# An attention-and-Hyena kernel on one core: issue order decided by a list scheduler for all five engines

## The chip, the cores and the metric

The kernel runs on one core of one Trainium2 chip. The metric is the device time of one execution in microseconds (us). The kernel before takes 576.78 us, the median of three runs from 569.41 to 578.04.

The engines are PE (TensorE: matrix products), PEld (the loading of its weights, which overlaps PE: in 451.6 us of the kernel before, the middle below, PE is busy for 376.4 us and PEld for 154.1, more than 451.6 together), DVE (VectorE), ACT (ScalarE), POOL (GpSimd) and SP (which issues most DMAs here).

## The reference, cut to what matters

```python
# q, k, v: [4 batches, 8 heads, 768, 64]
def _attn_ref(q, k, v, centroids):
    q_assign = argmax(normalised(q) @ normalised(centroids).T)     # 16 clusters
    k_assign = argmax(normalised(k) @ normalised(centroids).T)
    mask = q_assign[:, :, :, None] == k_assign[:, :, None, :]
    scores = where(mask, q @ k.T / 8, -1e9)
    attn = exp(scores - max);  attn = attn / (sum(attn) + 1e-9)
    return attn @ v

def _moe_ref(x, w_proj, filter_fft, w_out):    # "Hyena" below
    x1, x2, x3 = split(x @ w_proj)             # 512 -> 3 * 512
    x2_conv = irfft(rfft(x2) * rfft(filter_fft))
    return (x1 * x2_conv * x3) @ w_out
```

(The `einsum` and `matmul` calls are written as `@`.) The heads' outputs, side by side, are the `x` of the second part. The transform is done by matrix products with tables of sines and cosines ("the tables").

Four kinds of work follow. *Routing* finds the clusters of eight groups (a group is half a batch's heads). *Attention* has 16 pairs of heads with six steps each, thus 96 steps; a step is two score products, two exponentials on ACT, eight value matmuls on PE and two running sums on DVE. A *denominator* closes each pair. *Hyena* runs once for each of the four batches, when that batch's attention is done. Routing and Hyena are laid between the attention steps as *filler*.

## The kernel before

The kernels use PSUM, into which PE writes, as eight banks. The pools take two pairs of banks for scores, one pair for the values and two single banks for all filler:

```python
    psS = ctx.enter_context(tc.tile_pool(name="psS", bufs=2, space=PSUM))
    psO = ctx.enter_context(tc.tile_pool(name="psO", bufs=1, space=PSUM))
    psF = ctx.enter_context(tc.tile_pool(name="psF", bufs=2, space=PSUM))
    # ... (cut)
    def bank():
        return psF.tile([128, 512], F32, name="pf")
    # ... (cut)
        def scores(self, sk, hp):
            K = 80 if hp == 0 else 128
            sps = psS.tile([128, 2, 512], F32, name="ps")
            for ch in range(2):
                nc.tensor.matmul(sps[:, ch, :384], ...)                # cut
            # ... (cut)
            nc.scalar.activation(p[:, :S]..., sps[:, :, :384], Act.Exp, scale=0.125)
```

A filler group is a handful of matmuls into one bank, and then a copy out of it. This is the first of Hyena's:

```python
        for m in range(3):
            for e in range(2):
                ps = bank()
                for kt in range(ND):
                    nc.tensor.matmul(ps, uvf[:, e, kt, ts(m, 128)], wpj[:, kt, DM:2 * DM],
                                     start=(kt == 0), stop=(kt == ND - 1))
                nc.scalar.copy(uv2[:, e, m], ps)
                yield
```

Only PE's order is laid down by hand. Twelve steps share the filler that stands ready at their start, by counting:

```python
    for i, (n, pr, sk) in enumerate(steps):
        # ... (cut: which filler is added)
        left = sum(f[1] for f in fill)
        nf = -(-left // (12 - w)) if left else 0
        # ... (cut)
        scores(i + 1, 0)
        emit((nf + 1) // 2)
        scores(i + 1, 1)
        emit(nf // 2)
        if sk == 0 and i:
            pairs[steps[i - 1][:2]].finish()      # the denominator, through DRAM
        pairs[n, pr].values(sk)
```

The softmax here doesn't subtract the row's maximum and nothing guards it: scores larger than these inputs give would overflow.

Of the kernel before, what the change touches and what calls it, by code (L numbers as in the profile page):

```python
# [2 lines left out]

# [15 lines left out]










@with_exitstack  # L30
def kernel(
# [13 lines left out]
    B, H, S, D = q.shape  # L45
    NC = centroids.shape[1]
    DM = moe_w_proj.shape[0]
    assert (B, H, S, D, NC) == (4, 8, 768, 64, 16)
    assert DM == H * D
    NT = S // 128  # L50
    HS = S // 2
    ND = DM // 128
    BIG = 262144.0
    EPS = 1e-30

    consts = ctx.enter_context(tc.tile_pool(name="consts", bufs=1))
    psS = ctx.enter_context(tc.tile_pool(name="psS", bufs=2, space=PSUM))
    psO = ctx.enter_context(tc.tile_pool(name="psO", bufs=1, space=PSUM))
    psF = ctx.enter_context(tc.tile_pool(name="psF", bufs=2, space=PSUM))
    dram = ctx.enter_context(tc.tile_pool(name="dram", bufs=2, space=bass.MemoryType.DRAM))  # L60

    def bank():
        return psF.tile([128, 512], F32, name="pf")


    raw = ctx.enter_context(tc.tile_pool(name="raw", bufs=4))
    vraw = ctx.enter_context(tc.tile_pool(name="vraw", bufs=2))
    qk_raws, v_raws = {}, {}

    def load_qk(n, pr, j):  # L70
        if n < 2 * B:
            tl = qk_raws[n, pr, j] = raw.tile([128, NT, 2, D], F32, name="qkraw")
            for hp in range(2):
                nc.sync.dma_start(tl[:, :, hp], (q, k)[j][n // 2, 4 * (n % 2) + 2 * pr + hp].rearrange(
                    "(p t) d -> p t d", t=NT))

    def load_v(b, g):
        vv = v_raws[b, g] = vraw.tile([128, 4, 384], F32, name="vraw")
        nc.sync.dma_start(vv, v[b, 4 * g:4 * g + 4].rearrange("h (p t) d -> p h (t d)", t=NT))

    for z in range(4):
        load_qk(0, z // 2, z % 2)
    load_v(0, 0)


    ident = consts.tile([128, 128], F32)
    make_identity(nc, ident)
    identb = consts.tile([128, 128], BF16)
    nc.vector.tensor_copy(identb, ident)
    ones32 = consts.tile([128, 32], F32)  # L90
    nc.gpsimd.memset(ones32, 1.0)

    cbd = consts.tile([128, 4, 32], F32)
    nc.gpsimd.memset(cbd, 0.0)
    cen = ctx.enter_context(tc.tile_pool(name="cen", bufs=1))
    c = cen.tile([128, D], F32)
    nc.scalar.dma_start(c, centroids.rearrange("h c d -> (h c) d"))
    c2 = cen.tile([128, D], F32)
    nc.vector.tensor_tensor(c2, c, c, op=Alu.mult)
    ss = cen.tile([128, 1], F32)  # L100
    nc.vector.tensor_reduce(ss, c2, axis=AX, op=Alu.add)
    nc.vector.tensor_scalar(ss, ss, 1e-30, None, op0=Alu.max)
    s0 = cen.tile([128, 1], F32)
    nc.scalar.activation(s0, ss, Act.Sqrt)

    s1 = cen.tile([128, 1], F32)
    nc.vector.reciprocal(s1, s0)
    nc.vector.tensor_tensor(s1, s1, ss, op=Alu.mult)
    nc.vector.tensor_tensor(s1, s1, s0, op=Alu.add)
    nc.vector.tensor_scalar(s1, s1, 0.5, 1e-6, op0=Alu.mult, op1=Alu.add)  # L110
    nc.vector.reciprocal(s1, s1)
    cn = cen.tile([128, D], F32)
    nc.vector.tensor_scalar(cn, c, s1, None, op0=Alu.mult)
    cps = bank()
    nc.tensor.transpose(cps[:D, :128], cn, ident)
    cv = cps[:D, :128].rearrange("d (r e c) -> d r e c", r=4, e=2)
    nc.vector.tensor_copy(cbd[:D, :, :NC], cv[:, :, 0])
    nc.vector.tensor_copy(cbd[D:, :, NC:], cv[:, :, 1])


    mka = consts.tile([128, 1], F32)
    mkb = consts.tile([128, 1], F32)
    for g in range(4):
        nc.gpsimd.memset(mka[32 * g:32 * g + 32], BIG if g % 2 == 0 else 1.0)
        nc.gpsimd.memset(mkb[32 * g:32 * g + 32], -BIG if g % 2 == 0 else 0.0)

    revc = consts.tile([128, 48, NC], BF16)
    nc.gpsimd.iota(revc, pattern=[[0, 48], [-1, NC]], base=NC, channel_multiplier=0,
                   allow_small_or_imprecise_dtypes=True)



    NSET = 2
    augs = [[[[consts.tile([128, S], BF16, name=f"aug{i}{pr}{hp}{j}") for j in range(2)]
              for hp in range(2)] for pr in range(2)] for i in range(NSET)]
    for i in range(NSET):
        for pr in range(2):
            for j in range(2):
                nc.gpsimd.memset(augs[i][pr][1][j][:D], 0.0)


    NP = 6
    pbuf = [consts.tile([128, S + 4], F32, name=f"p{i}") for i in range(NP)]
    for p in pbuf:
        nc.gpsimd.memset(p[:, S:S + 1], EPS)
    np_ = [0]

    wpj = consts.tile([128, ND, 3 * DM], BF16)
    wout = consts.tile([128, ND, DM], BF16)


    fw = [consts.tile([128, 3, HS], BF16, name=f"fw{i}") for i in range(2)]
    inv = consts.tile([128, 6, HS], BF16)
    hm = consts.tile([128, 3, 4, DM], BF16)

    def forward_tables():
        with tc.tile_pool(name="tabw", bufs=1) as tab:
            s0 = tab.tile([128, 1], F32)
            nc.gpsimd.iota(s0, pattern=[[0, 1]], base=0, channel_multiplier=6,
                           allow_small_or_imprecise_dtypes=True)  # L160
            nc.vector.tensor_scalar(s0[64:], s0[64:], -383.0, None, op0=Alu.add)
            kc = tab.tile([128, 2, HS], F32)
            sh = tab.tile([128, 2, HS], F32)
            for i in range(2):
                nc.gpsimd.iota(kc[:, i], pattern=[[0, 2], [2, 192]], base=i, channel_multiplier=0,
                               allow_small_or_imprecise_dtypes=True)
                nc.gpsimd.memset(sh[:, i, :192], 192.0)
                nc.gpsimd.memset(sh[:, i, 192:], 0.0)
            nc.gpsimd.memset(kc[:, 0, 192:193], 384.0)
            nc.gpsimd.memset(sh[:, 0, 192:193], 192.0)  # L170
            MAGIC = 12582912.0
            for m in range(3):
                sm = tab.tile([128, 1], F32, bufs=2)
                nc.vector.tensor_scalar(sm, s0, float(2 * m), None, op0=Alu.add)
                n = tab.tile([128, 2, HS], F32, bufs=2)
                nc.vector.scalar_tensor_tensor(n, kc, sm, sh, op0=Alu.mult, op1=Alu.add)
                r = tab.tile([128, 2, HS], F32, bufs=2)
                nc.vector.tensor_scalar(r, n, 1.0 / S, MAGIC, op0=Alu.mult, op1=Alu.add)
                nc.vector.tensor_scalar(r, r, MAGIC, -float(S), op0=Alu.subtract, op1=Alu.mult)
                nc.vector.tensor_tensor(n, n, r, op=Alu.add)  # L180
                for i in range(2):
                    nc.scalar.activation(fw[i][:, m], n[:, i], Act.Sin, scale=2.0 * math.pi / S)

    def tables():

        with tc.tile_pool(name="tab", bufs=1) as tab:
            flo = tab.tile([128, 3, DM], F32)
            fhi = tab.tile([128, 3, DM], F32)
            fv = moe_filter_fft.rearrange("(w p m e) d -> w e p m d", w=2, p=64, m=3, e=2)
            for e in range(2):  # L190
                nc.sync.dma_start(flo[64 * e:64 * e + 64], fv[0, e])
                nc.sync.dma_start(fhi[64 * e:64 * e + 64], fv[1, e])

            for j in range(6):
                tp = bank()[:].bitcast(BF16)
                for m in range(3):
                    cols = (0, 192, 0, 192, 128, 320)[j]
                    o = tp[:, m * 128:(m + 1) * 128]
                    if j < 4:
                        nc.tensor.transpose(o, fw[j // 2][:, m, cols:cols + 128], identb)  # L200
                    else:
                        for i in range(2):
                            nc.tensor.transpose(o[64 * i:64 * i + 64], fw[i][:, m, cols:cols + 64], identb)
                nc.scalar.copy(inv[:, j], tp[:, :HS])
                yield
            fu = tab.tile([128, 3, DM], BF16)
            fd = tab.tile([128, 3, DM], BF16)
            nc.vector.tensor_tensor(fu, flo, fhi, op=Alu.add)
            nc.vector.tensor_tensor(fd, flo, fhi, op=Alu.subtract)

            w1 = tab.tile([128, 1], F32)
            wz = tab.tile([128, 1], F32)
# [256 lines left out]
    xu = {}  # L469
# [97 lines left out]
```

## Time and profile before

One profiled execution spans 571.7 us. I divide every execution at two instants, both read from the timeline: the start of the first value matmul, and the end of the last. The *head* lies before, the *middle* between, the *tail* behind.

| part | us | PE busy | PE idle |
|---|---|---|---|
| head | 56.7 | 18.9 | 37.8 |
| middle | 451.6 | 376.4 | 75.3 |
| tail | 63.4 | 37.1 | 26.3 |

The first lines come from the page of the kernel before: the span, each engine's busy time, PE's busy tenths and its granted clock in 40 slices of 14.3 us, and the chain that ended last by engine.

```profile
span 571.7 us, 6805 instructions
...
PE 432.3 (76%) x2405; PEld 179.9 (31%) x2417; DVE 339.7 (59%) x459; ACT 257.6 (45%) x432; POOL 177.1 (31%) x168
...
PE   5015997987689669977689768969689778965675
...
PEclk9657999989699899989699899998799897996998
...
PE 45%; DVE 25%; DMA 10%; issue 8%; SPq 5%; ACT 5%; POOL 2%; POOLq 0%; DVEq 0%; ACTq 0%
```

PE is the busiest engine and yet idle for a quarter of the span. The slices show the holes: one at the start (5015), then sixes and sevens again and again. The granted clock stands at 7 tenths or less in eight slices, and in seven of these PE is busy for 6 tenths or less (in the second to fourth, 0, 1 and 5 tenths busy at a clock of 6, 5 and 7). The reverse does not hold everywhere: in the 15th and the 24th PE is at 6 tenths and the clock at 9.

The next view of the kernel before gives the three parts. Its columns are the window, its length, then busy time and number of instructions of PE, PEld, DVE, ACT and POOL, the granted clock, the DMA share and GB/s.

```profile
0.00:56.68 56.68, 18.86 (x114) 10.63 (x115) 29.41 (x52) 16.24 (x30) 20.12 (x56) 0.73 0.68 153
56.68:508.30 451.62, 376.35 (x2122) 154.14 (x2134) 288.59 (x372) 227.34 (x376) 139.88 (x100) 0.94 0.22 59
508.30:571.70 63.40, 37.07 (x174) 15.13 (x176) 21.70 (x36) 14.07 (x27) 17.14 (x12) 0.89 0.09 35
```

Last, four lines of the waits of the kernel before: who waited for whom, us in total, how many times, the longest.

```profile
ACT p_160 L329 <- PE ps L325: 71.0, 31, 20.3
...
PE pf L391 <- DVE uT L379: 32.1, 5, 8.4
...
PE pf L240 <- DVE fu L208: 14.5, 1, 14.5
...
PE ps L325 <- DMA aug_137<-ohT: 9.8, 3, 3.7
```

PE waits for the filter sum (`fu`) in the head, for Hyena's input (`uT`) in the middle and the tail, and for the mask rows (`aug`) in the middle. The exponentials that use one buffer waited 71 us for scores: PE was with filler, or idle. Two lines of the timeline of the kernel before (start, duration, engine, operation) gave the measure for what an attention step costs where PE is fully fed:

```profile
484.11 0.50 PE L325 MATMUL ps<-aug_144,aug_145 80*128 80x384 bf16 x2
...
486.31 0.50 PE L325 MATMUL ps<-aug_144,aug_145 80*128 80x384 bf16 x2
```

From one step's scores to the next step's is 2.20 us.

### The profile page before, as it was taken

The numbers are of one execution on the slowest core, as the hardware profiler recorded it, in microseconds if no ns is written. First come the engines' busy times: TensorE is split into PE (matmuls) and PEld (weight loads), VectorE is DVE, ScalarE is ACT, GpSimd is POOL, SyncE is SP. The second block draws the span as 40 slices with busy tenths as digits, with TensorE's granted clock in tenths as the row PEclk, the third lists the DMA queues.
The fourth block names the chain that finished last, engine by engine and source line by source line (L and its number), as shares of the span: only waits on it lengthen the run. The fifth ranks groups of instructions, "written<-read, shape, count | busy, mean of one in ns | idle before, by whom it ended". The sixth has DMA issues, their size and how long they took to land.

```text
span 571.7 us, 6805 instructions
## 1 busy us (share of the span) xinstructions
PE 432.3 (76%) x2405; PEld 179.9 (31%) x2417; DVE 339.7 (59%) x459; ACT 257.6 (45%) x432; POOL 177.1 (31%) x168
## 2 busy tenths in 40 slices
PE   5015997987689669977689768969689778965675
PEld 3012433323234224423234224324233233322331
DVE  2907886986369534796269533696368631872630
ACT  4131766746344327746344326736354324742122
POOL 9400704405060133425060233516251221000621
PEclk9657999989699899989699899998799897996998
DMA  8970405315010205315011115312000002010002
GB/s 207 227 165 6 112 20 135 85 42 141 28 29 29 60 10 166 85 43 141 28 29 30 31 39 163 88 37 63 28 1 29 15 1 112 29 31 28 1 1 110
DMA packets 67538, 37.48 MB, mean 66 GB/s; under 512 B 56944, under 2 KB 62640, under 8 KB 67504
## 3 DMA queue, kind: packets, MB, share of 16 engines
q1 hardware_dynamic: 66304, 34.91, 22.4%
q0 software_dynamic: 1056, 2.10, 2.0%
q8 instruction: 19, 0.31, 0.2%
q14 instruction: 15, 0.12, 0.1%
q10 hardware_dynamic: 144, 0.03, 0.0%
HBM read 31.06 MB, written 6.49 MB: 66 GB/s over the span
## 4 chain that ended last, share of the span: by engine, by line
PE 45%; DVE 25%; DMA 10%; issue 8%; SPq 5%; ACT 5%; POOL 2%; POOLq 0%; DVEq 0%; ACTq 0%
PE o L340 15%; PE ps L325 8%; PE pf L391 5%; PE pf L447 4%; DMA rb<-dr 4%; PE pf L412 3%; DVE tm L401 3%; SPq L308 3%; PE pf L262 2%; PE pf L275 2%; PE pf L359 2%; DMA dr<-dn 2%; PE pf L428 2%; DVE uT L380 2%; DMA fhi<-in_moe_filter_fft_dram 1%
## 5 line engine op out<-in xcount | busy, mean ns | idle before, releaser
L329 ACT ACTIVATE p_160<-ps 128x768 f32<-128x768 f32 x32 | 26.0, 812 | 76.1 <-PE ps L325 71.0
L412 PE MATMUL pf<-xT,wpj 128*128 128x384 bf16 x256 | 50.7, 326 | 12.7 <-ACT od L431 5.7
L340 PE MATMUL o<-p_165,vraw 128*64 128x385 f32 (+1 forms) x128 | 55.0, 558 | 0.0
L340 PE MATMUL o<-p_164,vraw 128*64 128x385 f32 (+1 forms) x128 | 55.0, 558 | 0.0
L391 PE MATMUL pf<-wpj,uT 128*128 128x512 bf16 x92 | 30.4, 476 | 32.4 <-DVE uT L379 32.1
L340 PE MATMUL o<-p_161,vraw 128*64 128x385 f32 (+1 forms) x128 | 48.2, 499 | 0.0
L340 PE MATMUL o<-p_163,vraw 128*64 128x385 f32 (+1 forms) x128 | 48.2, 499 | 0.0
L340 PE MATMUL o<-p_160,vraw 128*64 128x385 f32 (+1 forms) x128 | 48.2, 499 | 0.0
L340 PE MATMUL o<-p_162,vraw 128*64 128x385 f32 (+1 forms) x128 | 48.2, 499 | 0.0
L404 POOL TENSOR_TENSOR hy<-tm 128x512 bf16<-128x512 f32 x24 | 32.1, 1360 | 50.1 <-DVE tm L401 50.1
L401 DVE TENSOR_TENSOR tm<-pf,hm 128x512 f32<-128x512 f32 x48 | 30.0, 682 | 18.4 <-PE pf L240 11.3
L329 ACT ACTIVATE p_164<-ps 128x768 f32<-128x768 f32 x32 | 26.0, 812 | 31.9 <-PE ps L325 31.9
L412 PEld LDWEIGHTS <-wpj 128*128 128x128 bf16 x256 | 23.6, 97 | 40.6 <-issue 21.1
L447 PE MATMUL pf<-wout,hy 128*128 128x512 bf16 x92 | 26.4, 438 | 11.4 <-POOL hy L437 8.8
L393 ACT CAST hy<-pf 128x512 bf16<-128x512 f32 x24 | 14.1, 586 | 44.8 <-PE pf L391 44.7
L262 PE MATMUL pf<-ident,qkraw 128*128 128x128 f32 x192 | 33.0, 286 | 1.0 <-ACT qkT L264 0.8
L264 ACT COPY qkT<-pf 128x384 f32<-128x384 f32 x64 | 30.9, 486 | 4.8 <-PE pf L262 4.8
L329 ACT ACTIVATE p_162<-ps 128x768 f32<-128x768 f32 x32 | 26.2, 818 | 14.1 <-PE ps L325 14.1
L262 PEld LDWEIGHTS pf<-ident,qkraw 128*128 128x128 f32 x192 | 25.4, 147 | 8.3 <-ACT qkT L264 2.8
L428 PE MATMUL pf<-inv,hy 128*128 128x384 bf16 (+1 forms) x128 | 22.0, 326 | 7.2 <-DVE x_1550 L417 0.6
L329 ACT ACTIVATE p_163<-ps 128x768 f32<-128x768 f32 x32 | 26.4, 824 | 1.8 <-PE ps L325 1.4
L329 ACT ACTIVATE p_161<-ps 128x768 f32<-128x768 f32 x32 | 26.1, 816 | 0.6 <-PE ps L325 0.2
(477 smaller groups left out, 951.9 us busy)
## 6 DMA issues: line engine op xcount, KB each, us to landing
qkraw<-in_q_dram SPq DMA_DIRECT2D x32, 192.0 KB
qkraw<-in_k_dram SPq DMA_DIRECT2D x32, 192.0 KB
vraw<-in_v_dram SPq DMA_DIRECT2D x8, 768.0 KB
rb<-dr SPq DMA_DIRECT2D x32, 192.0 KB
out_dram<-tm SPq DMA_DIRECT2D x12, 512.0 KB
wpj<-in_moe_w_proj_dram POOLq DMA_DIRECT2D x1, 1536.0 KB, 11.7
flo<-in_moe_filter_fft_dram SPq DMA_DIRECT2D x2, 384.0 KB
fhi<-in_moe_filter_fft_dram SPq DMA_DIRECT2D x2, 384.0 KB
```

Source lines behind the costliest of these rows:

```text
L262: nc.tensor.transpose(tps[:, ts(t, 128)], qr[:, 3 * ch + t].rearrange("p h d -> p (h d)"), ident)
L264: nc.scalar.copy(qkT[z][:, ch], tps[:, :384])
L308: nc.sync.dma_start(augs[aset][pr][hp][j][64 - 16 * hp:80 - 16 * hp], ohT[r0:r0 + 16])
L325: nc.tensor.matmul(sps[:, ch, :384], self.aug[hp][1][:K, ts(sk, 128)], self.aug[hp][0][:K, ts(ch, 384)], start=True, stop=True)
L329: nc.scalar.activation(p[:, :S].rearrange("p (a b) -> p a b", a=2), sps[:, :, :384], Act.Exp, scale=0.125)
L340: nc.tensor.matmul(self.o[64 * hp:64 * hp + 64, ch, :384 + ch], vv[:, 2 * self.pr + hp, sk * D:(sk + 1) * D], pb[hp][sk][:, 384 * ch:384 * ...
L391: nc.tensor.matmul(ps, uvf[:, e, kt, ts(m, 128)], wpj[:, kt, DM:2 * DM], start=(kt == 0), stop=(kt == ND - 1))
L401: nc.vector.tensor_tensor(tm[r][:, cs], ps, hm[:, i, 2 * r + cs], op=Alu.mult)
L404: nc.gpsimd.tensor_tensor(y[:, i, r], tm[r][:, 0], tm[r][:, 1], op=Alu.add)
L412: nc.tensor.matmul(ps[:, :384], wpj[:, kt, off + dt * 128:off + dt * 128 + 128], xT[:, kt, ts(ch, 384)], start=(kt == 0), stop=(kt == ND - 1))
L428: nc.tensor.matmul((pe, po)[e][:, :384], y[lo:hi, i, cs, ts(dt, 128)], inv[lo:hi, row], start=(n == 0), stop=(n == 3))
L447: nc.tensor.matmul(ps, y2[:, kt, ts(2 * tt + e, 128)], wout[:, kt], start=(kt == 0), stop=(kt == ND - 1))
```

## The change

The intent: the kernel is written as a list of operations, each with a due time, the keys that it reads and writes, and a duration for each engine that may do it. A list scheduler places them on a model of the core (engines, PSUM banks, one DMA rate, and a rule that keeps marked operations of DVE and POOL from being planned at the same time) before anything is emitted. All five engines then issue in the order of the planned starts. Along with that, the mathematics loses half of the sine-table work, most casts leave POOL, copies out of PSUM go to ACT or DVE as the plan has it, the filter loads come early, and the last denominator is spread by matmuls and not through DRAM.

The diff, cut to its core:

```diff
+    def place(self, free0, banks_for, switch=0.1, wait=0.1, rate=215e3):
+        free = dict(free0)
+        bank_free = [0.0] * 8
...
+            o.start, o.on = t, e
+            free[e] = t + d
+            busy[e] += d
+            o.end = t + d
...
+        return sorted(self.ops, key=lambda o: (o.start, o.seq))
...
+def banks_for(bank, free, st, o):
+    if bank.cls == "score":
+        two = min(((0, 1), (2, 3)), key=lambda p: max(free[p[0]], free[p[1]]))
+        return two if max(free[two[0]], free[two[1]]) < 1e8 else None
+    if bank.cls == "o":
+        return (4, 5) if max(free[4], free[5]) < 1e8 else None
+    allowed = [6, 7]
+    if st.score == 0 and bank.cls == "head":
+        allowed += [0, 1, 2, 3, 4, 5]
+    elif st.score == st.scores:
+        allowed += [0, 1, 2, 3]
+        if st.odone == st.otiles:
+            allowed += [4, 5]
...
+    def ap(h):
+        return T.ps[h.ids[0] // 2][:, h.ids[0] % 2]
...
+                op(EV512, lambda e, m=m, e_=e_, h=h: copy(e, T.uv2[:, e_, m], ap(h)), due + 1, r=[h],
+                   w=[("uv2", e_, m)], free=[h])
...
+            op(("POOL", 1.8), lambda e, dt=dt, xb=xb: T.nc.gpsimd.tensor_tensor(
+                T.y2[:, dt], T.yy[:].rearrange("p t c -> p (t c)"), T.x3[xb][:].rearrange("p a b -> p (a b)"),
...
-    psS = ctx.enter_context(tc.tile_pool(name="psS", bufs=2, space=PSUM))
-    psO = ctx.enter_context(tc.tile_pool(name="psO", bufs=1, space=PSUM))
-    psF = ctx.enter_context(tc.tile_pool(name="psF", bufs=2, space=PSUM))
...
+    _, order = build(T)
...
+    T.ps = [pp.tile([128, 2, 512], F32, name=f"ps{i}") for i in range(4)]
...
+    ctx.enter_context(tc.manual_schedule())
+    for o in order:
+        o.fn(o.on)
```

## The prediction

> **What bounds the kernel now.** TensorE, when it is fed. The slices: PE busy 76% of 571.7 us, granted clock 0.91; DVE 59%, ACT 45%, POOL 31%. Attention's first value matmul starts at 56.75 us (timeline): the tables stand ahead of it in PE's order, and PE waits 14.5 us for the filter sum, whose loads were issued only at 34.7 us (waits). Then 450 us of attention with filler, PE busy 375 us; last a tail of 65 us, PE busy 38 us.
>
> The holes are the cost. In each middle batch (130, 129, 106 us) PE waits 6 to 8 us for uT (the denominator's trip through DRAM), 2 to 4 us for the next group's mask rows, 2 us for POOL. From 196 to 218 us Hyena runs alone while the exponentials starve (one slot's waited 71 us for scores in all). Holes also slow PE: after the 3.7 us wait at 250.7 us a value matmul took 0.90 us, against 0.54 warm. [...]
>
> **What the change does.** Nearly the same mathematics, ordered in advance on all five engines. It shares PSUM copies between ACT and DVE, moves bf16 casts off POOL (80 to 90 us there by the groups), halves the sine-table work, loads the filters early, takes the tables out of attention's way, spreads Hyena between attention steps, and replaces the last DRAM trip by matmuls.
>
> **PE work, from cadences in fully busy, clock 1.00 stretches of before.** One attention step 2.20 us (484.11 to 486.31) x96 = 211. Routing 8x0.33 + 2x0.83 + 2x0.33 + 0.42 = 5.4, x7 = 38. Denominators 0.78x16 = 12.5. Hyena (4-matmul groups 0.87 and 0.65, inverse 1.1) 29.4, x4 = 118. Before the last Hyena: about 350 us.
>
> DVE and ACT together need about 630 us for two engines (597 busy plus casts taken over), so they stay under PE except in the first 28 or so steps, where no Hyena exists yet: there they need about 2.6 us each per step against PE's 2.8; I take 3.1.
>
> - Head: attention from about 27 us instead of 56.75 (head loads run at about 210 GB/s; q, k, v and filters must pass): -29.
> - Middle: 350 us at 95%, plus 8 us for the DVE-limited start: 376 instead of 450: -74.
> - Tail: denominator on PE 8, Hyena 29.4, bubbles 6, last product, eviction, store 6: 49 instead of 65: -16.
>
> 27 + 376 + 49 = 452. I predict **450 us**, range 425 to 485. Chances: faster by over 2% 0.96, within 2% 0.02, slower 0.02.
>
> **What would show it.** First value matmul at 26 to 31 us; from there to the last Hyena PE over 92% busy at clock 0.97 or more; PE's waits for uT, mask rows and POOL under 1 us each; POOL busy near 90 us; tail under 52 us. Total PE busy falls only to some 400 us.
>
> **What would make it wrong.** In-order engines stall wherever the model's durations are off, and pass the stall on; DVE beside POOL is the likeliest place. Sums took 0.95 us alone, 1.30 to 1.65 beside POOL [...]. If DVE binds the whole middle: 480. SP too issues in one order, so a late denominator can hold back loads. If the schedule is tighter than I think: 430.

What the trace of the kernel before shows is this: after the wait of 3.73 us that began at 250.7 us, the granted clock was 0.54 from 254.43 to 258.00 us and 1.00 in the 4 us after that. Beside the casts of POOL from 59.4 to 70.1 us eight sums took 0.95 to 1.57 us, and with POOL idle (485.5 to 487.3 us) two took 0.95 and 0.96 us.

## The result, and the profile after

The changed kernel takes 522.06 us, the median of four runs from 521.10 to 524.02. The ratio to the kernel before is 0.912, with a 95% interval of 0.9053 to 0.9187. A ratio here is always the mean time of one kernel's fast runs over that of the other's fast runs of the same rounds, so it is not quite the ratio of the medians. The change is faster, but 72 us slower than predicted and outside the range.

The page of the changed kernel, with the same lines (a slice is now 13.0 us):

```profile
span 519.7 us, 6779 instructions
...
PE 427.9 (82%) x2444; PEld 179.7 (35%) x2444; DVE 355.5 (68%) x556; ACT 274.5 (53%) x420; POOL 90.5 (17%) x93
...
PE   3777899999979787797978888888978799969944
...
PEclk9966999999999999999999999999999999979997
...
PE 59%; DVE 21%; ACT 9%; issue 5%; DMA 2%; POOL 1%; POOLq 0%; DVEq 0%; ACTq 0%; SPq 0%
```

The long holes have gone (PE's longest gap in the middle was 7.97 us and is 1.77), and with them the clock's dips in the middle (a mean of 0.94 before, 1.00 now). But PE is not full: from the twelfth slice on it stands mostly at seven and eight tenths, evenly, without a deep hole anywhere. From the sixth slice to the eleventh it is full. Hyena's filler begins just where that ends.

The three parts of the changed kernel, columns as before:

```profile
0.00:44.76 44.76, 24.98 (x135) 14.33 (x135) 33.00 (x69) 23.55 (x42) 12.59 (x45) 0.85 0.96 207
44.76:456.99 412.23, 358.32 (x2084) 145.58 (x2083) 295.83 (x445) 234.47 (x348) 61.59 (x38) 1.00 0.23 60
456.99:519.70 62.71, 44.62 (x227) 19.78 (x227) 26.66 (x44) 16.51 (x30) 16.27 (x11) 0.89 0.13 51
```

The middle lasts 412.2 us for 358.3 us of PE work: 53.9 us of idle time, at a granted clock of 1.00, with DVE and ACT far from full as well (295.8 and 234.5 us). No engine is busy throughout. Something makes PE wait a little, very often. Four lines of the changed kernel's waits, of which the last two are PE's:

```profile
ACT p L464 <- PE ps L460: 46.6, 42, 4.4
...
ACT uv L203 <- PE ps L587: 18.8, 14, 3.1
...
PE ps L587 <- ACT uv L203: 7.0, 10, 0.9
...
PE ps L661 <- POOL y L649: 5.2, 2, 2.8
```

The waits that troubled the kernel before are small: PE waits under 1 us for `uT`, and for POOL 5.2 us (last line), all of it in the tail. All exponentials together wait 46.6 us (first line), where those of one buffer had waited 71 us. The second and third lines are the clue, for they are two sides of one thing: ACT's copy waits for the product (14 times, 18.8 us), and PE's product waits for the copy (10 times, up to 0.9 us). The timeline of the changed kernel shows them, in the first products of a Hyena (L587 is the product, L203 the copy; the bracket gives the idle time before and who ended it; lines of other engines and of weight loads are left out):

```profile
263.45 1.90 PE L587 MATMUL ps<-wpj,uT 128*128 128x512 bf16 x8
...
265.39 0.58 ACT L203 CAST uv<-ps 128x512 bf16<-128x512 f32 x1 [1.84 <-PE ps L587]
...
266.03 1.02 PE L587 MATMUL ps<-wpj,uT 128*128 128x512 bf16 x4 [0.67 <-ACT uv L203]
...
267.09 0.59 ACT L203 CAST uv<-ps 128x512 bf16<-128x512 f32 x1 [1.11 <-PE ps L587]
267.73 1.02 PE L587 MATMUL ps<-wpj,uT 128*128 128x512 bf16 x4 [0.68 <-ACT uv L203]
...
268.79 0.58 ACT L203 CAST uv<-ps 128x512 bf16<-128x512 f32 x1 [1.11 <-PE ps L587]
269.42 1.02 PE L587 MATMUL ps<-wpj,uT 128*128 128x512 bf16 x4 [0.67 <-ACT uv L203]
```

With two banks I expected PE to fill one while ACT empties the other. That is not what happens. PE fills both (eight matmuls, 263.45 to 265.35). Only then, at 265.39, does the first copy start, though its own four matmuls ended near 264.5 (in the split version below, a first copy starts 1.07 us after the first matmul). From there product and copy take turns strictly: 1.02 us, 0.58 us, 1.02 us. A group comes every 1.70 us. Each engine stands idle while the other works, as if there were one bank.

The pairs tell when it starts. The first five pairs begin 17 to 21 us apart in the changed kernel (at 44.8, 65.9, 83.2, 102.4 and 119.8 us), and 16 to 19 us apart in the split version of the first experiment below (at 43.1, 62.5, 78.9, 96.5 and 113.1 us): no great difference. From the seventh to the fifteenth pair, where Hyena's filler stands between the steps, the changed kernel goes from 166.2 to 411.3 us and the split version from 152.6 to 357.5: 245.1 against 204.9 us.

### The profile page after: what moved, and what is told of

Same layout as the page of the kernel before. It is cut to its first block, busy times and chain, and to the rows that moved or that the text cites. A ratio compares the mean times of both kernels' runs of the same rounds, so it can differ in the third digit from the quotient of the medians.

```text
span 519.7 us, 6779 instructions
## 1 busy us (share of the span) xinstructions
PE 427.9 (82%) x2444; PEld 179.7 (35%) x2444; DVE 355.5 (68%) x556; ACT 274.5 (53%) x420; POOL 90.5 (17%) x93
## 4 chain that ended last, share of the span: by engine, by line
PE 59%; DVE 21%; ACT 9%; issue 5%; DMA 2%; POOL 1%; POOLq 0%; DVEq 0%; ACTq 0%; SPq 0%
PE ps L475 19%; PE ps L616 8%; PE ps L460 7%; PE ps L661 5%; PE ps L587 4%; PE ps L369 4%; DVE acc L485 4%; DVE tm L600 3%; PE ps L639 3%; PE ps L498 2%; PE ps L387 2%; ACT uv L203 2%; DVE x L623 2%; ACT qkT L203 1%; DMA qkraw<-in_q_dram 1%
## 5 line engine op out<-in xcount | busy, mean ns | idle before, releaser
L464 ACT ACTIVATE p<-ps 128x768 f32<-128x768 f32 x192 | 149.5, 812 | 63.5 <-PE ps L460 46.6
L475 PE MATMUL ps<-p,vraw 128*64 128x385 f32 x768 | 147.0, 503 | 0.4 <-ACT osb L490 0.2
L485 DVE TENSOR_TENSOR acc<-acc,p 128x768 f32<-128x768 f32 x128 | 125.9, 1024 | 6.9 <-ACT p L464 6.7
L460 PE MATMUL ps<-aug,aug 128*128 128x384 bf16 (+1 forms) x384 | 85.7, 331 | 6.6 <-ACT p L464 5.1
L475 PEld LDWEIGHTS ps<-p,vraw 128*64 128x64 f32 x768 | 47.3, 137 | 66.1 <-issue 63.1
L616 PE MATMUL ps<-xT,wpj 128*128 128x384 bf16 x256 | 48.5, 326 | 14.2 <-DVE x L205 3.4
L604 POOL TENSOR_TENSOR y<-tm 128x512 bf16<-128x512 f32 x24 | 36.3, 1520 | 120.2 <-DVE tm L600 119.6
L369 PE MATMUL ps<-ident,qkraw 128*128 128x128 f32 x192 | 36.0, 312 | 22.7 <-DMA qkraw<-in_q_dram 9.0
L649 POOL TENSOR_TENSOR y<-yy,x 128x768 bf16<-128x768 f32 x16 | 32.6, 2035 | 120.2 <-DVE yy L645 79.7
L460 PEld LDWEIGHTS <-aug 128*128 128x128 bf16 (+1 forms) x384 | 33.4, 98 | 50.8 <-issue 37.5
L587 PE MATMUL ps<-wpj,uT 128*128 128x512 bf16 x96 | 23.3, 379 | 7.8 <-ACT uv L203 7.0
L203 ACT COPY qkT<-ps 128x384 f32<-128x384 f32 x44 | 20.5, 482 | 16.4 <-PE ps L369 12.5
L203 ACT COPY x<-ps 128x384 f32<-128x384 f32 x24 | 11.5, 479 | 33.0 <-PE ps L616 20.0
L203 ACT COPY ob<-ps 128x512 f32<-128x512 f32 x23 | 12.8, 591 | 22.1 <-PE ps L661 15.5
L203 ACT CAST uv<-ps 128x512 bf16<-128x512 f32 x21 | 12.2, 585 | 23.2 <-PE ps L587 18.8
```

Source lines behind the costliest of these rows:

```text
L203: T.nc.scalar.copy(out, in_)
L369: T.nc.tensor.transpose(ap(h)[:, ts(t, 128)], T.qkraw[s][:, 3 * ch + t].rearrange("p h d -> p (h d)"), T.ident)
L460: T.nc.tensor.matmul(two(h)[:, ch, :384], ag[1][:K, ts(sk, 128)], ag[0][:K, ts(ch, 384)], start=True, stop=True)
L464: ex = op(("ACT", .82 + (1.28 if first[0] is None else 0)), lambda e, h=h, s=s: T.nc.scalar.activation(T.p[s][:, :S].rearrange("p (a b) -> ...
L475: T.nc.tensor.matmul(o[64 * hp:64 * hp + 64, ch, :385], T.vraw[aset][:, 2 * pr + hp, sk * D:(sk + 1) * D], T.p[slots[hp, sk]][:, 384 * ch: ...
L485: T.nc.vector.tensor_tensor(T.acc[hp], x, T.p[slots[hp, sk]][:, :S], op=Alu.add)
```

## The experiments

**Theory A.** Suppose that the waits on PSUM are kept per tile. The changed kernel declares its PSUM as four tiles of two banks each, so the filler banks 6 and 7 are the halves of one tile. A copy out of one half would then wait for whatever PE has issued into the other half, and PE's next group for that copy: two banks would act as one. The kernel before declared them as two tiles. The planner, whose model has eight separate banks, knows nothing of it.

**Rival B.** In-order engines with wrong durations in the model: a stall on DVE beside POOL is passed on to PE. This was the risk that the prediction named.

**Rival C.** Two banks are simply too few for the filler that the new plan puts between attention steps.

One look at the built program needs no run. I counted the waits there whose releasing instruction had touched only the other half of the waiting instruction's tile. The changed kernel has 245: 76 of ACT on PE, 59 of DVE on PE, 64 of PE on DVE and 46 of PE on ACT, all on PSUM tiles (59 more, between ACT and DVE, are not in this count). That shows that the waits are there, not what they cost.

### e1_split: the two filler banks as two tiles

Nothing but the declaration changes. The plan is the same; the order of instructions on all five engines was compared and is the same, one for one, and the filler's tiles lie in banks 6 and 7 in both programs. (The text gives the turn-taking group as 2.0 us; the trace has 1.70.)

```diff
     def ap(h):
-        return T.ps[h.ids[0] // 2][:, h.ids[0] % 2]
+        return T.bank(h.ids[0])
...
-    T.ps = [pp.tile([128, 2, 512], F32, name=f"ps{i}") for i in range(4)]
+    T.ps = [pp.tile([128, 2, 512], F32, name=f"ps{i}") for i in range(3)]
+    T.one = [pp.tile([128, 512], F32, name=f"psf{i}") for i in range(2)]
+    T.bank = lambda i: T.ps[i // 2][:, i % 2] if i < 6 else T.one[i - 6][:]
```

(The same replacement is made where Hyena's inverse takes its two banks.)

> The same planned order as the changed kernel, but the two PSUM banks of the filler (6 and 7) are tiles of their own instead of halves of one two-bank tile. Theory A (the changed kernel loses its time because a copy out of one half of the two-bank tile is made to wait for the next matmul group into the other half, so the two banks work as one): the 2.0 us per-group lockstep of the Hyena projections (1.70 us per group of 4 matmuls in place of 0.87) goes, pairs with Hyena filler take about 26 us again, last value matmul at about 405 to 412 us instead of 455.5, total 468 to 480 us. Theory B (in-order engines stall because the model's durations are off [...]): under 2% change, 512 to 524 us. Theory C (two filler banks are too few at real latencies, whatever the tiles): 505 to 520 us.

Measured: 465.00 us (464.07 to 465.38), ratio 0.8098 (0.8036 to 0.8159). That is 57 us less than the changed kernel, and correct. It is also a little better than Theory A's numbers (468 to 480 us, and the last value matmul at 405 to 412 us, where it came at 399). The page of the split version:

```profile
span 463.6 us, 6827 instructions
...
PE 422.0 (91%) x2444; PEld 180.3 (39%) x2444; DVE 355.7 (77%) x556; ACT 274.7 (59%) x420; POOL 90.1 (19%) x93
...
PE   2866999999999999999999999999997999699846
```

Its middle and tail, columns as before:

```profile
43.10:399.28 356.18, 350.30 (x2084) 145.57 (x2083) 297.12 (x447) 234.55 (x348) 61.50 (x38) 0.99 0.27 69
399.28:463.60 64.32, 46.87 (x227) 20.33 (x227) 26.60 (x44) 16.70 (x30) 16.27 (x11) 0.84 0.12 50
```

PE's idle time in the middle falls from 53.9 to 5.9 us. The middle shrinks by 56.0 us, of which 48.0 are idle time and 8.0 are busy time (358.3 to 350.3). DVE, ACT and POOL do the same work in it to within 1.3 us. Head and tail differ by under 2 us from the changed kernel's. The same Hyena products, in the timeline of the split version:

```profile
233.83 5.35 PE L587 MATMUL psf<-wpj,uT 128*128 128x512 bf16 x24
...
234.90 0.59 ACT L203 CAST uv<-psf 128x512 bf16<-128x512 f32 x1 [1.04 <-PE psf L587]
...
235.76 0.58 ACT L203 CAST uv<-psf 128x512 bf16<-128x512 f32 x1 [0.28 <-PE psf L587]
...
236.63 0.58 ACT L203 CAST uv<-psf 128x512 bf16<-128x512 f32 x1 [0.28 <-PE psf L587]
```

All 24 matmuls of the six groups run without a gap, and a copy starts every 0.87 us beside them. Copies of 0.58 us out of one bank run beside an unbroken 5.35 us of matmuls into the two. The same order with the two banks in one tile cost 57 us more.

Theory A is shown: nothing else was changed, and the effect has the size of the loss in the middle. Rival C is out, since two banks suffice for the same plan. Rival B can claim at most the 5.9 us that are left in the middle. 43 waits on the other half remain in this version, in head and tail, where the other six banks serve filler.

### e2_shortpool: POOL's products cut short

If DVE and POOL disturb each other, nearly taking away POOL's work should win the time back. From the second batch on, POOL's two operations of Hyena, a sum and a product, take only 32 columns, so the output is wrong (relative error 1.24).

```diff
+        W_, W2_ = (512, 768) if b == 0 else (32, 32)
...
-                    T.y[:, i, r], T.tm[r][:, 0], T.tm[r][:, 1], op=Alu.add), ...
+                    T.y[:, i, r, :W_], T.tm[r][:, 0, :W_], T.tm[r][:, 1, :W_], op=Alu.add), ...
...
-                T.y2[:, dt], T.yy[:].rearrange("p t c -> p (t c)"), T.x3[xb][:].rearrange("p a b -> p (a b)"),
+                T.y2[:, dt, :W2_], T.yy[:].rearrange("p t c -> p (t c)")[:, :W2_],
+                T.x3[xb][:].rearrange("p a b -> p (a b)")[:, :W2_],
```

> Wrong result on purpose: the changed kernel in its planned order, with POOL's sums and products of batches 1 to 3 cut to 32 columns (about a tenth of their time), all waits kept. Theory B (DVE against POOL): POOL's 69 us of these operations and the lengthened sums on DVE (mean 1.02 us against 0.95) go, 490 to 505 us. Theory A: the middle hardly moves, only the tail loses POOL's last product and sums (some 4 to 8 us): 512 to 520 us.

Measured: 506.94 us (504.44 to 507.68), ratio 0.8826 (0.8766 to 0.8886), from the changed kernel's 522.06. It lies between the numbers of the two theories, so the parts must decide. Middle and tail of this run:

```profile
43.60:451.40 407.80, 357.44 (x2084) 145.28 (x2083) 288.12 (x444) 234.53 (x348) 38.08 (x38) 1.00 0.23 61
451.40:502.70 51.30, 40.02 (x227) 18.42 (x227) 24.93 (x44) 16.31 (x30) 2.51 (x10) 1.00 0.16 62
```

The middle falls by only 4.4 us (412.2 to 407.8), and DVE's busy time in it by 7.7 us. The tail falls by 11.4 us (62.7 to 51.3); 4.6 us of these are PE's busy time, at a granted clock of 1.00 against 0.89. POOL hardly matters for the disputed loss, but it matters in the tail, where its products stand in the chain of the last Hyena. I had not expected that size.

### b1_joined: the kernel before with its two filler banks in one tile

The same thing in the opposite direction and in the other kernel, whose order is by counting.

```diff
-    psF = ctx.enter_context(tc.tile_pool(name="psF", bufs=2, space=PSUM))
+    psF = ctx.enter_context(tc.tile_pool(name="psF", bufs=1, space=PSUM))
+    pf2, turn = psF.tile([128, 2, 512], F32, name="pf"), [0]
...
     def bank():
-        return psF.tile([128, 512], F32, name="pf")
+        turn[0] += 1
+        return pf2[:, turn[0] % 2]
```

> The kernel before with its two filler banks joined into one two-bank tile, halves taken in turn, as the change did. Theory A: the same false waits appear here; PE's order is fixed and the filler comes in bursts, so it loses 25 to 60 us: 600 to 635 us. Theories B and C say nothing of tiles: 565 to 580 us.

Measured: 749.86 us (748.14 to 754.30), ratio 1.3079 (1.2986 to 1.3171), against 575.51 of the kernel before on the same chip. Middle and tail of this run:

```profile
68.20:637.74 569.54, 425.63 (x2131) 158.81 (x2134) 280.75 (x371) 228.73 (x375) 120.85 (x100) 0.87 0.17 47
637.74:746.30 108.56, 59.86 (x176) 19.37 (x176) 22.02 (x36) 14.05 (x27) 17.09 (x12) 0.58 0.05 19
```

The direction is right and the size far above the text: 174 us, not 25 to 60. The built program has 332 waits on the other half of the filler's tile, counting those between ACT and DVE, where the kernel before has none. In the middle PE is idle for 143.9 us (569.5 less 425.6) against 75.3 before, and PE's busy time grows by 49.3 us for the same work. The tail, which is filler alone, grows from 63.4 to 108.6 us. The granted clock goes with it, from 0.94 to 0.87 in the middle and from 0.89 to 0.58 in the tail. One stretch of the tail, with columns as before, and two lines of PE's timeline in it:

```profile
664.80:739.90 75.10, 47.71 (x136) 15.71 (x136) 14.99 (x26) 8.08 (x16) 14.66 (x10) 0.50 0.02 9
...
680.87 1.44 PE L414 MATMUL pf<-xT,wpj 128*128 128x384 bf16 x4 [0.57 <-ACT x L417]
683.02 1.44 PE L414 MATMUL pf<-xT,wpj 128*128 128x384 bf16 x4 [0.72 <-DVE x L419]
```

In these 75 us the granted clock was 0.50 though no gap of PE was longer than 1.9 us, and in two stretches of the middle (405.4 to 443.0 and 572.7 to 610.2 us), also at 0.50, none was longer than 2.1 us. PE was 64 to 68% busy there. In the changed kernel's middle, where the gaps are some 0.7 us long (1.77 us at most) and strewn, and PE is 86.9% busy, the clock stayed at 1.00, and PE was idle for 53.9 us all the same: a granted clock of 1.00 does not say that PE is fed. Where between the two the clock gives way, no run here shows. My estimate had counted the waits and left out the slower clock (0.87 and 0.58, above) and the chain behind each wait. Of the 174.6 us by which the profiled span grew, 82.2 are PE's longer busy time for the same work and 92.4 its longer idle time. How each divides between waits, clock and chains I did not separate.

### e3_head: attention's first inputs before everything else

The head was also mis-predicted: 44.8 us, not 27. In the split version, the filter loads and the next group's q and k are held back until the first group's mask rows have gone out.

```diff
-    qslot, loads = {}, []
+    qslot, loads, masks = {}, [], []
...
-  ... due, w=[("qkraw", s, hp)], byts=196e3, kind="load")
+  ... due, w=[("qkraw", s, hp)], byts=196e3, kind="load", after=masks if n else ())
...
-  ... 16.0, w=[("f", w_, e_)], byts=393e3, kind="load")
+  ... 16.0, w=[("f", w_, e_)], byts=393e3, kind="load", after=masks)
```

(The score products are also chained in their own order; without that, the planner ran into a state from which it could place nothing.)

> The split version (465.0 us), planned again with the filter loads and all later q and k loads held back until the first group's mask rows are issued. If my prediction's head term was right in kind (attention starts late only because those loads stand ahead of the mask rows, and an earlier start is won time): first value matmul at 30 to 36 us instead of 43, total 455 to 460 us. If the head is bound by the loads of the second group and of the filters as well (what is not moved before attention stalls it later): first value matmul as early, but the third pair starts later than in the split version (78.9 us), total 470 to 485 us.

Measured: 474.45 us (473.21 to 475.55), ratio 0.8289 (0.8214 to 0.8365): 9 us slower than the split version, which ran on the other chip (the intervals of the two ratios do not meet). The middle of this run:

```profile
34.80:409.07 374.27, 358.92 (x2124) 150.06 (x2132) 309.51 (x463) 237.92 (x356) 67.19 (x42) 0.99 0.30 76
```

The first value matmul comes at 34.8 us, 8.3 us sooner than in the split version, but the third pair starts at 93.6 us and not at 78.9. The early start is paid back with more than interest. Between the last value matmuls of the second pair and the first of the third (61.1 to 93.6 us) PE does the filters' transform and the second group's routing, whose loads were put off, and is idle for 9.3 us. In the changed kernel's head the DMA share is 0.96 at 207 GB/s: the head is full of loading, and this other order of loads only shifted the debt.

### e4_tail: the last Hyena's product on POOL or DVE, as the plan sees fit

This takes the split version and e2's finding on the tail, with right results. It was run on another chip.

```diff
-            op(("POOL", 1.8), lambda e, dt=dt, xb=xb: T.nc.gpsimd.tensor_tensor(
+            op({"POOL": 1.8, "DVE": .95} if last else ("POOL", 1.8), lambda e, dt=dt, xb=xb: (
+                T.nc.vector if e == "DVE" else T.nc.gpsimd).tensor_tensor(
```

> The split version with the last batch's four products of y2 free to go to DVE as well as POOL. The shortened POOL operations gave the changed kernel 11 us in its tail; four products of 1.8 us are the larger part of it on the chain that ends last. Tail from the last value matmul 65.8 us falls to 60 to 63, total 458 to 463 us, the middle unchanged. If POOL's part of the tail is hidden by the inverse matmuls: 463 to 466 us.

Measured: 459.86 us (457.22 to 461.41), ratio 0.8037 (0.7970 to 0.8103). The time is as expected; the tail is shorter than expected. The tail of this run:

```profile
398.98:455.40 56.42, 41.47 (x225) 18.85 (x227) 30.42 (x48) 16.63 (x30) 9.07 (x7) 0.97 0.14 56
```

The tail falls from 64.3 to 56.4 us in the profiles. Not all of this can be put down to the change: the profiled run is the fastest of the four, 2.6 us under the median, and 5.4 of the 7.9 us are PE's busy time for the same work (46.87 to 41.47 us), at a granted clock of 0.97 against 0.84. What part of the clock was chance is not shown. Another wait stands in the same place: at the end of attention the last four sums run beside one of POOL's products. The timeline of the split version:

```profile
398.20 5.17 DVE L485 TENSOR_TENSOR acc<-acc,p 128x768 f32<-128x768 f32 x4
...
398.43 2.38 POOL L649 TENSOR_TENSOR y<-yy,x 128x768 bf16<-128x768 f32 x1 [3.23 <-DVE yy L645]
```

Four sums take 5.17 us, the second of them alone 2.56. One takes 0.95 us undisturbed in the same trace, and in e2, where POOL's product is cut short, the same four take 3.56 us (from 450.30). The last denominator waits for them. In these traces both are slower side by side: POOL's product lies wholly inside those 5.17 us and takes 2.38 us, against 1.80 us where it is shortest.

### e5_cal: the planner's durations set to the measured ones

The remaining claim of Rival B: in the split version the model's durations still differ from the traces'. An exponential lasts 0.81 us, but the next starts 0.70 us after it; PE's results are recorded some 0.165 us after its next instruction could start (value matmuls recorded as 0.49 us follow each other every 0.32 to 0.33 us, in the kernel before too); transposes are shorter (0.34 us, planned 0.52) and value groups longer (1.35 us, planned 1.28).

```diff
-            free[e] = t + d
+            free[e] = t + d - {"ACT": .11, "DVE": .085}.get(e, 0.0)
...
-            o.end = t + d
+            o.end = t + d + .165 * (e == "PE")
...
-            op(("PE", 1.28), pv, due, ...
+            op(("PE", 1.35), pv, due, ...
```

(And seven more durations of PE, from the trace.)

> The split version planned again with durations measured from the trace: PE results land 0.165 us after the next matmul may start, ACT and DVE take the next operation 0.11 and 0.085 us before the last has landed, value groups 1.35 us, transposes 0.34 us. Theory B's second half (a better model gives a better order): 450 to 460 us. Theory A (the order was good, only false waits spoilt it): within 1% of the split version, 461 to 469 us.

Measured: 468.78 us (466.89 to 470.06), ratio 0.8195 (0.8129 to 0.8260), no better than the split version's 465.00 on the other chip. Head, middle and tail are 45.9, 360.0 and 61.6 us. This one calibration won nothing, so the durations in the model were good enough for this: what the model lacked was not a duration but a dependence.

### e6_best: no filler in the other half of a pair, anywhere

Taken from e4, this removes the waits that were left (42 in e4's program, 43 in the split version's). Outside attention, filler may use only one half of each two-bank tile.

```diff
-        allowed += [0, 1, 2, 3, 4, 5]
+        allowed += [0, 2, 4]
     elif st.score == st.scores:
-        allowed += [0, 1, 2, 3]
+        allowed += [0, 2]
         if st.odone == st.otiles:
-            allowed += [4, 5]
+            allowed += [4]
```

> The split version with the tail of e4_tail, and with filler in the head and the tail taking one half only of each score or value tile, so that no copy shares a tile with the next matmul group there either. Theory A: the few false waits that are left (43 in the program) go, worth 1 to 3 us beyond e4_tail: 456 to 461 us.

Measured: 456.01 us (455.46 to 456.38), ratio 0.7973 (0.7914 to 0.8032), correct, and no wait on another half is left in the built program. It is the fastest of all, 66 us under the changed kernel. Against e4 on the same chip it wins 3.9 us of medians, and its slowest run (456.38) is faster than e4's fastest (457.22); the step is under 1%, with fewer banks in use.

## Why the prediction was right or wrong

The three terms of the prediction's sum against the runs (us):

| | head | middle | tail | span |
|---|---|---|---|---|
| predicted | 27 | 376 | 49 | 452 |
| before | 56.7 | 451.6 | 63.4 | 571.7 |
| changed | 44.8 | 412.2 | 62.7 | 519.7 |
| e1_split | 43.1 | 356.2 | 64.3 | 463.6 |
| e2_shortpool | 43.6 | 407.8 | 51.3 | 502.7 |
| e6_best | 42.1 | 356.4 | 55.2 | 453.7 |

**The step that failed: "Middle: 350 us at 95%, plus 8 us for the DVE-limited start: 376".** The work of 350 us was right, almost to the number: PE's busy time in the middle of the split version is 350.3 us. So close a match is partly luck, for the 350 held about 5 us of output products (six groups at 0.87 us) that in fact ran in the tail. The 8 us for a DVE-limited start were not needed: in the split version PE is idle for only 0.7 us between 43 and 170 us. The 95% was wrong for the changed kernel. PE was busy for 86.9% of the changed kernel's middle (358.3 of 412.2) and for 98.3% of the split version's (350.3 of 356.2). I took "two filler banks" for two things that wait independently, because they are banks 6 and 7 in the built program and two banks in the plan. The line that joins them was in the diff: `T.ps` is declared as four tiles of two banks. I read the addresses in it and not what a wait is attached to. In the runs that line costs 57 us, which is most of the 72 us between the prediction and the result.

**The head was mis-sized: 27 predicted, 44.8 measured.** The sum reckoned with q, k, v and the filters at about 210 GB/s. The rate was right (207 GB/s, the DMAs 96% busy), the amount was not: 44.76 us at that rate are 9.3 MB, 27 us at 210 GB/s are 5.7 MB. In the changed kernel's timeline the first group's mask rows are issued only from 29.8 us on, while the two projection weights (2 MB, issued at 27.0 and 28.0 us) are loading; the third group's q and k follow. Last, PE's planned order puts a transpose of the third group's q before the next score product, and PE waits for that load:

```profile
43.32 0.87 PE L369 MATMUL ps<-ident,qkraw 128*128 128x128 f32 x3 [3.75 <-DMA qkraw<-in_q_dram]
```

e3 shows that putting the filters and the second group off brings attention forward to 34.8 us and costs more afterwards. So this is not an idle head that the one other order tried would simply fill.

**The tail was mis-sized: 49 predicted, 62.7 measured.** Its term took only the last denominator and Hyena. It left out the previous batch's last output products, reckoned with the middle, which the changed kernel still had to run after the last value matmul (six groups, at 466 to 473 us), the last four sums, slower beside POOL (5.17 us in the split version, 3.56 in e2), and POOL's products inside the last Hyena. It also took PE at full clock, where the tail's was 0.89. Putting POOL's last products where the plan likes went with 7.9 us less in e4, and shortening them and those beside the sums with 11.4 us less in e2, the higher clock included in both.

**The errors of the terms partly cancel in the split version:** its middle is 20 us below the predicted 376 and its head and tail together 31 us above the predicted 76. That 463.6 us comes near 452 is therefore no proof of the terms.

The checks that the prediction named:

- First value matmul at 26 to 31 us: wrong, 44.76.
- PE over 92% busy before the last Hyena: wrong, 86.9%. Clock of 0.97 or more there: right, 1.00.
- PE's waits for `uT`, mask rows and POOL under 1 us each: right in the middle; 5.2 us for POOL in the tail.
- POOL busy near 90 us: right, 90.5.
- Tail under 52 us: wrong, 62.7.
- PE busy falls to some 400 us: wrong, 427.9 (25.0 in the head, 358.3 in the middle, 44.6 in the tail).
- The risk named, DVE beside POOL: real but small in the middle. A sum took 1.02 us on average against 0.95 alone, and e2 wins 4.4 us there.

Right was that the change is faster by over 2%, that it gains because the long holes close and the clock stays up (1.00 in the middle, 0.94 before), and that POOL and the DRAM trips leave PE's way.

What stays open: how the 174 us of b1 divide between waits, clock and chains, beyond the 82 us of busy and 92 us of idle time; what part of the shorter tails of e2 and e4 is the clock alone; and how much of the 5.9 us of idle time left in the middle of the split version belongs to which cause.

## What to carry to other kernels

Ask of every buffer what the waits are attached to, not only how many there are of it: in a kernel written with tiles as here, buffers that are to turn independently are better declared as separate tiles, even if they are adjacent halves of one array (as halves of one tile they cost 57 us in the changed kernel and 174 us in b1). Where two engines strictly take turns on what should be two buffers (product, copy, product, copy, with neither overlapping), look at the declaration before looking at durations. A scheduler's model is only as good as its dependences: here well-measured durations won nothing, and one undeclared dependence cost 57 us.
